# Layer 1 of the last two token blocks: eight of sixteen channel tiles by seven half products

## The chip, the core and the metric

The kernel runs on one core of a Trainium2 chip. The metric is the time of one execution on the device, in microseconds (us). The kernel before has a median of 338.77 us over three runs (338.13 to 338.88). A profile is one further execution with its trace.

## What is computed

Causal attention over 8 batches of 8 heads, 576 tokens and 64 features a head, with 16 beacon keys ahead of each sequence; then a low-rank mix along the sequence, and a two-layer perceptron on each token:

```python
scores = scale * np.matmul(q, k_all.transpose(0, 1, 3, 2))     # causal mask, softmax
x = softmax(scores) @ v_all                                    # (8, 576, 512) by tokens
h = x.transpose(0, 2, 1) @ U @ V                               # rank 32, along the sequence
u = x + h.transpose(0, 2, 1)
ch = np.maximum(u @ w_ch1, 0.0) @ w_ch2                        # 512 -> 2048 -> 512
return (u + ch).astype(np.float32)
```

Only the perceptron is touched: `u @ w_ch1` with the maximum is called layer 1 here, the product with `w_ch2` layer 2. Operands on the chip are 16-bit floats, sums are 32-bit.

## The kernel before

**Tiling.** The 8 x 576 = 4608 tokens go through the perceptron in nine blocks of 512 (`t` = 0 to 8). `uT` holds u with features on the partitions (4 tiles of 128), `w1` the weights of layer 1 (4 feature tiles by 2048 channels), so 16 channel tiles `dc` come out. Layer 1 of a block is 16 units (`g_unit`, L600): four matmuls of 128 weights by 512 tokens accumulate in one PSUM bank `gps` (L607), and the maximum with zero moves the bank into `gT` as 16-bit, on ScalarE for twelve of the units (L618) and on VectorE for the units 2, 5, 11 and 13 (L616).

**Layer 2** of blocks 1 to 8 is a 2 by 2 by 2 product of halves by seven products instead of eight (`product`, L627): `gT` is seen as four quarters (tokens halves of 256, channel halves of eight tiles), `sums` (L589) makes the four sums of quarters s1 to s4 on VectorE, `wt` holds four differences of `w2` quarters, and the seven products land in the banks A, F, B, C, D, E and D again, 16 matmuls of 256 columns each (L633), 112 for a block. Each product is two units (`c_unit`, L719). `SUMS` (L979) says after which unit each piece of the sums is issued. `after` (L668) joins the banks: one copy on ScalarE (L670), additions on VectorE (L654), the residual on GpSimd (also L654, `eng=nc.gpsimd`), and a store.

**Order.** Every engine's order is the order in which the program issues (`manual_schedule`). The units wait in one `queue`; `fill(n)` (L995) issues the next n of them between the steps of the attention, and with each unit it takes one entry of `coming` (L1004), a list of GpSimd's loads. For p = 12 to 31 (p is a pair of heads, four a batch) `long_slot` (L1198) writes out which scores, masks, attention products and units follow each other. After p = 31 `mix(B - 1)` (L1268) issues the rest of block 6 with the last mix, and the blocks 7 and 8, which are fed only then, run from L1273 on with nothing of the attention between them. `guard` (L813) and `guard_sum` (L825) check the softmax sums; `guard_sum` stands 22 units ahead of the end.

**Banks.** `pst` (L108) takes the bank that was emptied the longest time ago of eight; `emptying` gives one back.

**Staging.** `qk_tiles` (L253) takes two tiles of 6 KB a partition (`st0`, `st1`) from a pool with two buffers each: one batch's keys and queries lie there until they are turned by transposes on SyncE's queue. Batch 7's are the last.

Of the kernel before, what the change touches and what calls it, by code (L numbers as in the profile page):

```python
# [9 lines left out]
F16 = mybir.dt.float16  # L10
BF16 = mybir.dt.bfloat16
F32 = mybir.dt.float32
I32 = mybir.dt.int32
AF = mybir.ActivationFunctionType
ALU = mybir.AluOpType
# [3 lines left out]
P = 128  # L19
# [11 lines left out]
def kernel(  # L31
# [13 lines left out]
    nc = tc.nc  # L45
    B, H, S, D = q.shape
    Nb = beacon_k.shape[2]
    DM = H * D
    R = moe_U.shape[1]
    FF = moe_w_ch1.shape[1]  # L50
    NCC = DM // P
    NDC = FF // P
# [12 lines left out]
    TJ = 6  # L65
# [27 lines left out]
    stage = ctx.enter_context(tc.tile_pool(name="stage", bufs=2))  # L93
# [14 lines left out]
    def pst(shape, dtype, name):  # L108

        b = emptied.pop(0)  # L110
        t = psum.tile(shape, dtype, tag=f"bank{b}", name=name)
        bank_of[id(t)] = (b, t)
        return t

    def emptying(t):
        emptied.append(bank_of.pop(id(t))[0])
# [34 lines left out]
    w1 = const.tile([P, NCC, FF], F16, name="w1", tag="w1")  # L151
# [5 lines left out]
    plain = w1[:, NCC - 1, FF - P : FF]  # L157
# [4 lines left out]
    RING = 4 * S  # L162
    uT = const.tile([P, NCC, RING], F16, name="uT", tag="uT")
# [7 lines left out]
    HF, HC, HT = NDC // 2, DM // 2, 256  # L171
# [392 lines left out]
            for h in range(2) for o, x, y in ((t1, b12, b11), (t3, b22, b12), (t2, b22, t1), (t4, b21, t2))  # L564
        ]

    def fast_units(t0, dst, last=False):


        cell, banks, obs = {}, {}, {}  # L570
        cols = u_cols(t0, 512)

        def begin():
            t = gtp.tile([P, NDC * 512 + 3 * HF * HT], F16, name="gT", tag="gT")
            g = t[:, 0 : NDC * 512].rearrange("p (d t) -> p d t", t=512)
            s = t[:, NDC * 512 :].rearrange("p (i d t) -> p i d t", i=3, t=HT)
            cell["g"] = g
            cell["a"] = [g[:, 0:HF, 0:HT], g[:, HF:NDC, 0:HT], g[:, 0:HF, HT:512], g[:, HF:NDC, HT:512]]
            cell["s"] = [s[:, 0], s[:, 1], g[:, 0:HF, HT:512], s[:, 2]]
            ut = utp.tile([P, 4, DM], F16, name="ut", tag="ut")  # L580
            cell["u"] = ut
            cell["turns"] = [
                lambda cc=cc, at=at, o=o, w=w: nc.sync.dma_start_transpose(
                    out=ut[:, ds(o // P, w // P), ts(cc, P)], in_=uT[:, cc, ds(at, w)]
                )
                for cc in range(NCC) for at, o, w in cols
            ]
# [12 lines left out]
        def g_unit(k):  # L600
            if k == 0:
                begin()
            dc = order[k]
            g = pst([P, 512], F32, name="gps")
            for cc in range(NCC):
                for at, o, w in cols:
                    nc.tensor.matmul(  # L607
                        g[:, ds(o, w)], w1[:, cc, ts(dc, P)], uT[:, cc, ds(at, w)],
                        start=(cc == 0 and o == 0), stop=(cc == NCC - 1), skip_group_check=len(cols) > 1,
                    )  # L610
            if k % 2 and cell["turns"]:
                cell["turns"].pop(0)()
            for x in SUMS.get(k, ()):
                sums(*x)
            if k in (2, 5, 11, 13):
                nc.vector.tensor_scalar_max(out=cell["g"][:, dc, :], in0=g, scalar1=0.0)  # L616
            else:
                nc.scalar.activation(out=cell["g"][:, dc, :], in_=g, func=AF.Relu)  # L618
            emptying(g)

        b11, b21, b22 = w2[:, 0:HF, 0:HC], w2[:, HF:NDC, 0:HC], w2[:, HF:NDC, HC:DM]
        t1, t2, t3, t4 = (wt[:, i, :, :] for i in range(4))

        def pieces(bank):
            return [(0, 0, HC), (1, 0, P), (1, P, P)] if last and bank == "D" else [(0, 0, HC), (1, 0, HC)]
# [93 lines left out]
        def c_unit(k, j):  # L719
            bank = products[k][0]  # L720
            p = pieces(bank)[j]
            product(*products[k], *p)
            for x in SUMS.get(NDC + 2 * k + j, ()):
                sums(*x)
            if k == 6 and last:
                i, c0, w = p
                o = obs["12"][:, i, ds(c0, w)]
                add(o, banks["D", i, c0], cell["w12"][:, i, ds(c0, w)])
                store("12", 0, 1, i, c0, w)
                emptying(banks.pop(("D", i, c0)))  # L730
            elif j == len(pieces(bank)) - 1:
                after(k)

        units = [lambda k=k: g_unit(k) for k in range(NDC)]
        units += [lambda k=k, j=j: c_unit(k, j) for k in range(7) for j in range(len(pieces(products[k][0])))]
        return units

# [95 lines left out]
    NP = B * NH2  # L833
    NBLK = B * S // 512
    Ls, qTs, xbs = {}, {}, {}
    coming, storing = [], []

    def load_batch(b):
        if b < DT0:
            Ls[b] = qk_tiles()  # L840
            emit_loads(b, Ls[b], vss[b % 2])
        else:
            coming.append(lambda: v_beacon(beacon_v[b], vss[b % 2]))
            coming.extend(lambda j=j: v_tokens(v[b], vss[b % 2], ALLH, [j]) for j in range(NT))
# [114 lines left out]
    def av_of(p):  # L959
# [16 lines left out]
    LAG = 10  # L976
    HINT = 5
    FAST = 1
    SUMS = {  # L979
# [28 lines left out]
    def feed(b):  # L1008

        while state["t"] < NBLK and 512 * (state["t"] + 1) <= S * (b + 1):  # L1010
            t = state["t"]
            dst = lambda i, m, t=t: rows[ds(512 * t + P * i, m), :]
            if t < FAST:
                units, state["part"] = mlp_units(512 * t, 512, dst, t % 2, t > 0)
                if t == FAST - 1:
                    for i, u in zip(DIFFS, halves_of_w2()):
                        units[i] = lambda a=units[i], u=u: (a(), u())
            else:
                units = fast_units(512 * t, dst, t == NBLK - 1)
            queue.extend(units)  # L1020
            state["t"] += 1

# [39 lines left out]
    with tc.manual_schedule(engines={ENG.PE, ENG.Activation, ENG.DVE, ENG.SP, ENG.Pool}):  # L1062
# [9 lines left out]
        t0, sc = qkT_of(0), scores_of(0)  # L1072
# [35 lines left out]
        t2, t3 = qkT_of(2), qkT_of(3)  # L1108
# [17 lines left out]
        head, begin, rest = first_mix(xbs[0])  # L1126
        feed(0)
        part = state["part"]
# [121 lines left out]
        for p in range(NP1, NP):  # L1250
            b, c = divmod(p, NH2)
            if c == (1 if b >= DT0 else 0) and b + 1 < B:
                load_batch(b + 1)
            if c == (1 if b + 1 == DT0 else 2) and DT0 <= b + 2 < B:
                load_whole(b + 2)
            qk = qkT_of(p + 2) if P6 <= p and p + 2 < min(NP, DT0 * NH2) else []
            if p == P6:
                turn_x(b - 1)
                mix_between(b - 1)
            if c == 0 and DT0 <= b + 1 < B:  # L1260
                tr = turns(b + 1)
                fill_turns(tr, len(tr))
            if p < P6:
                play(third[c])
            else:
                long_slot(p, c, av_of(p), qk or [lambda: None] * 2)
# [60 lines left out]
    with tc.If(n_bad != 0, label="general"):  # L1327
        with tc.For_i(0, B, 1) as bi:
# [14 lines left out]
            for t0 in range(0, S, 512):  # L1343
                n = min(512, S - t0)
# [32 lines left out]
```

## Time and profile before

| | |
|---|---|
| median of 3 runs | 338.77 us |
| the profiled execution | 338.48 us |
| its span, first to last instruction | 336.8 us |
| granted TensorE clock, mean | 0.998 |
| block 7: layer 1, layer 2 | from 279.30, from 293.11 us |
| block 8: layer 1, layer 2 | from 305.34, from 319.35 us |
| last matmul ends | 331.6 us |

In the lines of the profile, PE is TensorE's matmuls, PEld its weight loads (they overlap PE), DVE is VectorE, ACT is ScalarE, POOL is GpSimd, SP is SyncE. A group line reads: line, engine, operation, output<-input, shapes, count | busy us, mean ns of one | idle time of the engine ahead of them and what ended it. A chain line reads: start, length, engine, tile, line, count. A timeline line reads: start, us, engine, line, operation, tiles, shapes, count, and in brackets the idle time before and its releaser. A window line reads: window, its length, busy us (and instructions) of PE, PEld, DVE, ACT and POOL, granted clock, share and rate of the DMA engines. The end of a matmul is modelled, so its own length (273 or 380 ns) is not the spacing of two matmuls; the spacing is read from starts.

### The profile page before, as it was taken

To read this page: it belongs to the slowest core of one execution; us is meant where nothing else is said; L and a number is where in the kernel's file an instruction comes from. 1 tells how busy PE (TensorE), PEld (TensorE's weight loads), DVE (VectorE), ACT (ScalarE), POOL (GpSimd) and SP (SyncE) were. 2 spreads that over 40 slices of the span, in tenths; PEclk is the share of its full clock that TensorE was granted. 3 is DMA by queue.
4 is the path that set the end of the run, shared out by engine and by line. 5 is a ranking of instruction groups with operands and counts; after the bars stand their busy time and mean duration, and the time that the engine had idled before them with its cause. 6 is when DMAs were issued, how large, how long until landed. Compare 5 with 4: busy or idle time off the path is not lost.

```text
span 336.8 us, 8862 instructions
## 1 busy us (share of the span) xinstructions
PE 328.0 (97%) x3542; PEld 216.5 (64%) x3542; DVE 234.3 (70%) x532; ACT 186.3 (55%) x403; POOL 141.2 (42%) x179
## 2 busy tenths in 40 slices
PE   8899999999999999999999999999999999999993
PEld 3565555555577557865688878656875675585493
DVE  6676888678897767775876587687776963733652
ACT  5957952888963677167716773577445303402500
POOL 8987714765335630786068706040140013013041
PEclk9999999999999999999999999999999999999999
DMA  7999999999999994999999999965123304004003
GB/s 165 142 182 155 174 200 189 200 186 137 85 167 137 130 182 89 139 206 144 166 112 157 153 120 123 138 127 101 35 80 81 70 33 140 16 33 140 18 33 102
DMA packets 150529, 41.98 MB, mean 125 GB/s; under 512 B 131280, under 2 KB 149904, under 8 KB 150480
## 3 DMA queue, kind: packets, MB, share of 16 engines
q0 software_dynamic: 87568, 18.18, 76.0%
q1 hardware_dynamic: 62688, 22.86, 36.2%
q8 instruction: 29, 0.48, 0.6%
q10 hardware_dynamic: 224, 0.30, 0.3%
q14 instruction: 20, 0.16, 0.2%
HBM read 37.45 MB, written 9.44 MB: 139 GB/s over the span
## 4 chain that ended last, share of the span: by engine, by line
PE 89%; ACT 5%; DVE 2%; DMA 1%; issue 0%; ACTq 0%; DVEq 0%
PE gps L607 32%; PE mpsD L633 8%; PE po L427 8%; PE sps L409 6%; PE mpsF L633 4%; PE cps L781 4%; PE mpsC L633 4%; PE mpsB L633 4%; PE mpsA L633 4%; PE gps L755 4%; PE mpsE L633 4%; ACT expt L376 2%; ACT w L376 2%; PE tps L298 1%; DMA stkq<-in_k_dram 1%; PE sps L370 1%
## 5 line engine op out<-in xcount | busy, mean ns | idle before, releaser
L607 PE MATMUL gps<-uT,w 128*128 128x512 f16 (+1 forms) x576 | 120.0, 356 | 0.2 <-ACT kT L907 0.2
L418 ACT ACTIVATE expt<-sps 128x496 f16<-128x496 f32 (+2 forms) x192 | 82.2, 547 | 41.6 <-PE sps L409 41.6
L654 POOL TENSOR_TENSOR ob<-ob,ut 128x512 f32<-128x512 f32 x30 | 36.0, 1203 | 143.9 <-DVE ob L654 134.7
L633 PEld LDWEIGHTS <-gT 128*128 128x128 f16 x912 | 85.5, 98 | 13.2 <-issue 2.9
L618 ACT ACTIVATE gT<-gps 128x512 f16<-128x512 f32 x96 | 57.2, 613 | 61.1 <-PE gps L607 55.8
L607 PEld LDWEIGHTS <-w 128*128 128x128 f16 x576 | 52.9, 98 | 46.4 <-issue 2.5
L596 DVE TENSOR_TENSOR gT<-gT 128x1024 f16<-128x1024 f16 (+2 forms) x88 | 45.3, 540 | 4.2 <-ACT gT L618 3.3
L240 POOL DMA_DIRECT2D vs<-in_v_dram x50 | 39.8, 811 | 14.0 <-DMA w<-in_moe_w_ch_dram 11.2
L427 PEld LDWEIGHTS <-expt 128*128 128x128 f16 x900 | 33.8, 98 | 9.8 <-issue 1.5
L616 DVE TENSOR_SCALAR gT<-gps 128x512 f16<-128x512 f32 x32 | 22.1, 690 | 24.2 <-PE gps L607 23.7
L427 PE MATMUL po<-vs,expt 128*128 128x65 f16 x900 | 36.4, 194 | 0.3
L348 DVE TENSOR_TENSOR expt<-expt,bigmask 128x768 f16<-128x768 f16 x54 | 33.9, 667 | 1.4 <-ACT expt L418 1.2
L436 DVE TENSOR_TENSOR xb<-po,rec 128x320 f16<-128x320 f32 x64 | 31.4, 491 | 2.2
L435 DVE RECIPROCAL rec<-po 128x5 f32<-128x5 f32 x64 | 12.1, 189 | 19.4 <-PE po L427 19.1
L409 PE MATMUL sps<-qT,kT 64*128 64x80 f16 (+4 forms) x288 | 22.6, 281 | 0.0
L376 ACT ACTIVATE expt<-sps 128x496 f16<-128x496 f32 (+2 forms) x48 | 20.4, 569 | 0.6 <-PE sps L370 0.6
L854 POOL DMA_DIRECT2D st<-in_q_dram x20 | 16.9, 871 | 7.7 <-DVE ob L654 6.8
L409 PEld LDWEIGHTS <-kT 64*128 64x128 f16 x288 | 10.3, 94 | 12.7 <-issue 8.2
L854 POOL DMA_DIRECT2D st<-in_k_dram x20 | 16.9, 859 | 0.6 <-DMA st<-in_q_dram 0.6
L755 PE MATMUL gps<-uT,w 128*128 128x512 f16 x64 | 16.2, 380 | 0.1
L633 PE MATMUL mpsE<-wt,gT 128*128 128x256 f16 x128 | 16.2, 273 | 0.0
L633 PE MATMUL mpsB<-wt,gT 128*128 128x256 f16 x128 | 16.1, 273 | 0.0
(121 smaller groups left out, 350.5 us busy)
## 6 DMA issues: line engine op xcount, KB each, us to landing
out_dram<-ob SPq DMA_DIRECT2D x35, 256.0 KB, 2.9
vs<-in_v_dram POOLq DMA_DIRECT2D x18, 128.0 KB, 6.6
w<-in_moe_w_ch_dram POOLq DMA_DIRECT2D x4, 512.0 KB, 6.2
w<-in_moe_w_ch_dram POOLq DMA_DIRECT2D x2, 1024.0 KB, 12.3
st<-in_k_dram POOLq DMA_DIRECT2D x12, 128.0 KB, 6.7
st<-in_q_dram POOLq DMA_DIRECT2D x12, 128.0 KB, 7.3
st<-in_k_dram POOLq DMA_DIRECT2D x4, 288.0 KB, 11.8
st<-in_q_dram POOLq DMA_DIRECT2D x4, 288.0 KB, 12.5
```

The lines of the kernel that those rows point to most:

```text
L240: nc.gpsimd.dma_start(out=dst[a : a + nq[j], j, :, :], in_=src[hs, ds(q0[j], nq[j]), :].rearrange("h p d -> p h d"))
L348: nc.vector.tensor_tensor(out=e, in0=e, in1=bigmask[:, :, :].rearrange("p (a b) x -> p a b x", b=2), op=ALU.min)
L376: nc.scalar.activation(out=ex[i][:, ds(AT[g], gw[g])], in_=ps[g, i][:, 0 : gw[g]], func=AF.Exp, scale=scale)
L409: nc.tensor.matmul(banks[i][:, ds(at0 + o, w)], kT(hp, c, ch), qT[hp, c, ds(qa, w)], start=True, stop=True, skip_group_check=len(unit) > 1,)
L418: nc.scalar.activation(out=at[p][3][i][:, ds(AT[g], gw[g])], in_=bank[:, ds(at0, gw[g])], func=AF.Exp, scale=scale)
L427: nc.tensor.matmul(po[:, j, :], ex[0 : nk[c], ds(blk[(c, j)], P)], vs[0 : nk[c], ds(c * H * E + h * E, E)], start=(c == 0), stop=(c == j),)
L596: nc.vector.tensor_tensor(out=o[:, ds(d0, n)], in0=x[:, ds(d0, n)], in1=y[:, ds(d0, n)], op=op)
L607: nc.tensor.matmul(g[:, ds(o, w)], w1[:, cc, ts(dc, P)], uT[:, cc, ds(at, w)], start=(cc == 0 and o == 0), stop=(cc == NCC - 1), skip_grou ...
L618: nc.scalar.activation(out=cell["g"][:, dc, :], in_=g, func=AF.Relu)
L633: nc.tensor.matmul(ps, a()[:, d, ds(P * i, P)], bm[:, d, ds(c0, w)], start=fresh and d == 0 and (i == 0 or key != bank), stop=d == HF - 1, ...
L654: eng.tensor_tensor(out=out, in0=x, in1=y, op=ALU.add)
L854: coming.append(lambda d=dst, s=src, a=m[j] - nq[j], n=m[j], j=j: nc.gpsimd.dma_start(out=d[a:n, j, :, :], in_=s[:, ds(q0[j], nq[j]), :].r ...
```

## The change

Layer 1 of the blocks 7 and 8 (`QUADS`) is issued in another form. Eight of the sixteen channel tiles stay whole units (`plain`, all emptied by ScalarE). The tiles 0 to 3 and 8 to 11 form two sets q = 0, 1: tiles 2q, 2q+1 with 8+2q, 9+2q. Each set is a 2 by 2 by 2 product of halves (features, channel pairs, tokens), made of seven half products of four matmuls of 256 columns (`half`). The sums of w1's quarters are made once, by GpSimd, as eight entries of `coming` at p = 29; the four differences of uT's quarters are made for each block by VectorE (`us`), and are shared by both sets. They lie in `lw`, two tiles that take the staging tiles' buffers; three ScalarE copies a set, in 32 bits, lie in `lk`, in the other buffers. The maximum with zero of these tiles is partly on ScalarE and partly on VectorE, in place. The order of the fifteen units of layer 1 is `slots`; the pieces of layer 2's sums are issued at other units (`late`, `after_g`). Blocks 0 to 6 are issued as before.

```diff
@@ -564,7 +564,32 @@
             for h in range(2) for o, x, y in ((t1, b12, b11), (t3, b22, b12), (t2, b22, t1), (t4, b21, t2))
         ]
 
-    def fast_units(t0, dst, last=False):
+    lq = {}
+
+    def quad_tiles():
+
+        t = [stage.tile([P, TJ * DM], F16, name=f"lw{i}", tag=f"st{i}") for i in range(2)]
+        lq["w"] = [x[:, 0 : 4 * 512].rearrange("p (k c f) -> p k c f", k=4, c=2) for x in t]
+        lq["t"] = [x[:, ds(4 * 512 + 512 * k, 512)].rearrange("p (c x) -> p c x", c=2) for x in t for k in range(2)]
+        f = [stage.tile([P, 3, 512], F32, name=f"lk{i}", tag=f"st{i}") for i in range(2)]
+        lq["k"] = [[x[:, k, :].rearrange("p (i x) -> p i x", i=2) for k in range(3)] for x in f]
+
+    def quad_weights(q):
+
+        def part(c0, d):
+            return w1[:, ds(c0, 2), ds(P * d, 2 * P)]
+
+        a11, a12, a21, a22 = part(0, 2 * q), part(2, 2 * q), part(0, HF + 2 * q), part(2, HF + 2 * q)
+        s1, s2, s3, s4 = (lq["w"][q][:, k, :, :] for k in range(4))
+        return [
+            lambda o=o, x=x, y=y, op=op: nc.gpsimd.tensor_tensor(out=o, in0=x, in1=y, op=op)
+            for o, x, y, op in (
+                (s1, a21, a22, ALU.add), (s2, s1, a11, ALU.subtract),
+                (s3, a11, a21, ALU.subtract), (s4, a12, s2, ALU.subtract),
+            )
+        ]
+
+    def fast_units(t0, dst, last=False, quads=False):
 
 
         cell, banks, obs = {}, {}, {}
@@ -617,6 +642,102 @@
             else:
                 nc.scalar.activation(out=cell["g"][:, dc, :], in_=g, func=AF.Relu)
             emptying(g)
+
+        def g_quads():
+
+            at = t0 % RING
+            b11, b12, b21, b22 = (uT[:, ds(c, 2), ds(at + x, HT)] for c in (0, 2) for x in (0, HT))
+            t1, t2, t3, t4 = lq["t"]
+            us = [
+                lambda o=o, x=x, y=y: nc.vector.tensor_tensor(out=o, in0=x, in1=y, op=ALU.subtract)
+                for o, x, y in ((t1, b12, b11), (t2, b22, t1), (t3, b22, b12), (t4, b21, t2))
+            ]
+            held = {}
+
+            def plain(k, dc):
+                if k == 0:
+                    begin()
+                g = pst([P, 512], F32, name="gps")
+                for cc in range(NCC):
+                    nc.tensor.matmul(
+                        g, w1[:, cc, ts(dc, P)], uT[:, cc, ds(at, 512)], start=cc == 0, stop=cc == NCC - 1
+                    )
+                nc.scalar.activation(out=cell["g"][:, dc, :], in_=g, func=AF.Relu)
+                emptying(g)
+
+            def half(q, bank, a, b, fresh):
+                if fresh:
+                    held[q, bank] = pst([P, 2, HT], F32, name="qps" + bank)
+                for i in range(2):
+                    for c in range(2):
+                        nc.tensor.matmul(
+                            held[q, bank][:, i, :], a(c, i), b[:, c, :], start=fresh and i == 0 and c == 0,
+                            stop=c == 1, skip_group_check=True,
+                        )
+
+            def of_w1(c0, d):
+                return lambda c, i: w1[:, c0 + c, ts(d + i, P)]
+
+            def of_lw(q, k):
+                return lambda c, i: lq["w"][q][:, k, c, ts(i, P)]
+
+            def copied(q, k):
+                nc.scalar.activation(out=lq["k"][q][k], in_=held[q, "A"], func=AF.Copy)
+
+            def summed(q, bank, k, d, x):
+                nc.vector.tensor_tensor(
+                    out=cell["g"][:, ds(d, 2), ds(x, HT)], in0=held[q, bank], in1=lq["k"][q][k], op=ALU.add
+                )
+
+            def relu(o):
+                nc.vector.tensor_scalar_max(out=o, in0=o, scalar1=0.0)
+
+            def step(q, n):
+                d, e = 2 * q, HF + 2 * q
+                if n == 0:
+                    half(q, "A", of_w1(0, d), b11, True)
+                    copied(q, 0)
+                    half(q, "F", of_w1(2, d), b21, True)
+                    summed(q, "F", 0, d, 0)
+                    emptying(held.pop((q, "F")))
+                    relu(cell["g"][:, ds(d, 2), 0:HT])
+                elif n == 1:
+                    half(q, "A", of_lw(q, 1), t2, False)
+                    copied(q, 1)
+                    half(q, "D", of_lw(q, 0), t1, True)
+                elif n == 2:
+                    half(q, "A", of_lw(q, 2), t3, False)
+                    copied(q, 2)
+                    summed(q, "D", 2, e, HT)
+                else:
+                    half(q, "A", of_w1(2, e), t4, False)
+                    nc.scalar.activation(out=cell["g"][:, ds(e, 2), 0:HT], in_=held[q, "A"], func=AF.Relu)
+                    emptying(held.pop((q, "A")))
+                    half(q, "D", of_lw(q, 3), b22, False)
+                    summed(q, "D", 1, d, HT)
+                    emptying(held.pop((q, "D")))
+                    relu(cell["g"][:, :, HT:512].rearrange("p (h d) t -> p h d t", h=2)[:, :, ds(d, 2), :])
+
+            slots = [4, 12, 5, (0, 0), (1, 0), (0, 1), (1, 1), 13, (0, 2, 1, 2), 6, 14, (0, 3), (1, 3), 7, 15]
+            late = {12: ((0, 4, 3),), 13: ((1, 4, 3), (2, 4, 3)), 14: ((0, 0, 4), (1, 0, 4))}
+
+            def unit(k, slot):
+                if isinstance(slot, int):
+                    plain(k, slot)
+                else:
+                    for i in range(0, len(slot), 2):
+                        step(slot[i], slot[i + 1])
+                if k < len(us):
+                    us[k]()
+                if k % 2 and cell["turns"]:
+                    cell["turns"].pop(0)()
+                for x in late.get(k, ()):
+                    sums(*x)
+
+            return [lambda k=k, slot=slot: unit(k, slot) for k, slot in enumerate(slots)]
+
+        after_g = {0: ((0, 7, 1), (1, 7, 1)), 1: ((2, 0, 4), (2, 7, 1)), 2: ((3, 0, 4),), 3: ((3, 4, 4),)}
+        sums_at = after_g if quads else {k - NDC: x for k, x in SUMS.items()}
 
         b11, b21, b22 = w2[:, 0:HF, 0:HC], w2[:, HF:NDC, 0:HC], w2[:, HF:NDC, HC:DM]
         t1, t2, t3, t4 = (wt[:, i, :, :] for i in range(4))
@@ -720,7 +841,7 @@
             bank = products[k][0]
             p = pieces(bank)[j]
             product(*products[k], *p)
-            for x in SUMS.get(NDC + 2 * k + j, ()):
+            for x in sums_at.get(2 * k + j, ()):
                 sums(*x)
             if k == 6 and last:
                 i, c0, w = p
@@ -731,7 +852,7 @@
             elif j == len(pieces(bank)) - 1:
                 after(k)
 
-        units = [lambda k=k: g_unit(k) for k in range(NDC)]
+        units = g_quads() if quads else [lambda k=k: g_unit(k) for k in range(NDC)]
         units += [lambda k=k, j=j: c_unit(k, j) for k in range(7) for j in range(len(pieces(products[k][0])))]
         return units
 
@@ -976,6 +1097,7 @@
     LAG = 10
     HINT = 5
     FAST = 1
+    QUADS = (7, 8)
     SUMS = {
         8: [(0, 0, 4)], 9: [(1, 0, 4)], 10: [(2, 0, 4)], 12: [(3, 0, 4)],
         14: [(0, 4, 3)], 15: [(1, 4, 3)], 16: [(2, 4, 3)], 17: [(0, 7, 1), (1, 7, 1)],
@@ -1016,7 +1138,7 @@
                     for i, u in zip(DIFFS, halves_of_w2()):
                         units[i] = lambda a=units[i], u=u: (a(), u())
             else:
-                units = fast_units(512 * t, dst, t == NBLK - 1)
+                units = fast_units(512 * t, dst, t == NBLK - 1, t in QUADS)
             queue.extend(units)
             state["t"] += 1
 
@@ -1251,6 +1373,9 @@
             b, c = divmod(p, NH2)
             if c == (1 if b >= DT0 else 0) and b + 1 < B:
                 load_batch(b + 1)
+            if p == NP - 3:
+                quad_tiles()
+                coming.extend(quad_weights(0) + quad_weights(1))
             if c == (1 if b + 1 == DT0 else 2) and DT0 <= b + 2 < B:
                 load_whole(b + 2)
             qk = qkT_of(p + 2) if P6 <= p and p + 2 < min(NP, DT0 * NH2) else []
```

## The prediction

> **What bounds the kernel now.** I read the page first, then the end of the chain of waits in order of time, then busy time by windows for the two blocks that change.
>
> ```profile
> span 336.8 us, 8862 instructions
> PE 328.0 (97%) x3542; PEld 216.5 (64%) x3542; DVE 234.3 (70%) x532; ACT 186.3 (55%) x403; POOL 141.2 (42%) x179
> ...
> PE 89%; ACT 5%; DVE 2%; DMA 1%; issue 0%; ACTq 0%; DVEq 0%
> ```
>
> TensorE is busy for 97% of the span and is 89% of the chain that ends last. The part that the change touches is the end of that chain:
>
> ```profile
> 277.39 1.91 PE mpsD L633 x16
> 279.30 13.81 PE gps L607 x64
> 293.11 1.75 PE mpsA L633 x16
> ...
> 305.34 8.63 PE gps L607 x40
> 314.06 5.29 PE gps L607 x24
> 319.35 1.75 PE mpsA L633 x16
> ...
> 329.85 1.78 PE mpsD L633 x24
> ```
>
> From 277.39 us on every link is TensorE and each starts where the one before ends: 54 us in which nothing else decides. So a matmul that isn't issued there is worth its whole spacing, as long as no other engine becomes late. The windows show how much the others have in hand:
>
> ```profile
> 279.30:293.10 13.80, 13.80 (x66) 6.29 (x65) 6.89 (x11) 6.57 (x11) 1.53 (x2) 1.00 0.34 95
> 293.10:305.30 12.20, 12.20 (x114) 10.91 (x112) 5.52 (x11) 1.19 (x2) 3.15 (x3) 1.00 0.11 37
> ```
>
> In layer 1 of block 7 VectorE (6.89 us) and ScalarE (6.57 us) work half of the 13.80 us. In layer 2 the weight loads take 10.91 of 12.20 us and are still covered: PE shows no gap.
>
> **The spacing of matmuls.** 64 matmuls of 512 columns take 13.81 us: 0.2158 us each. The 112 of 256 columns in block 7's layer 2 run from 293.11 to 305.34: 12.23 / 112 = 0.1092 us each. That is more than half of 0.2158, by a little; the rest is a price per matmul, and the seven-for-eight trade pays it on more matmuls. Before, a set of four channel tiles is 16 matmuls of 512 columns, 16 x 0.2158 = 3.453 us. After, it is 7 x 4 = 28 of 256 columns, 28 x 0.1092 = 3.058 us. A set saves 0.395 us, a block 0.79 us, and the four sets 1.58 us. Break-even would be a spacing of 3.453 / 28 = 0.1233 us. The half products have the same shape, the same 16-bit weights of 128 columns and the same alternation inside one bank as layer 2's products, so I take 0.1092; below 0.1079 (half of 0.2158) no row goes, which would add 28 x 4 x 0.0013 = 0.15 us to the gain.
>
> A rule speaks against this. The Trainium skill, "TensorE: Matmul & The Clock Gate", section "Back-to-back issue gap", gives sustained spacings of 81 ns for 128 columns and 131 ns for 512; on the straight line between them 256 columns would be an estimate of 98 ns, a set would go from 16 x 131 = 2096 to 28 x 98 = 2744 ns, and four sets would lose 2.6 us. The trace's 215.8 ns for 512 columns contradicts it and agrees with the formula of the same section that the page calls isolated (N / 2.4 + 2.5 ns: 215.8 and 109.2), so the sum stands by the rows.
>
> **Does TensorE stay unbroken in layer 1?** Durations of the work that is added or moved:
>
> ```profile
> L618 ACT ACTIVATE gT<-gps 128x512 f16<-128x512 f32 x24 | 14.3, 597 | 35.9 <-PE gps L607 35.9
> L596 DVE TENSOR_TENSOR gT<-gT 128x1024 f16<-128x1024 f16 x10 | 6.8, 685 | 3.4 <-ACT gT L618 3.3
> L616 DVE TENSOR_SCALAR gT<-gps 128x512 f16<-128x512 f32 x8 | 5.5, 693 | 10.1 <-PE gps L607 10.1
> ...
> L596 DVE TENSOR_TENSOR gT<-gT 128x768 f16<-128x768 f16 x6 | 3.2, 555 | 0.3
> ...
> L596 DVE TENSOR_TENSOR gT<-gT 128x256 f16<-128x256 f16 x6 | 1.6, 290 | 0.1
> L654 DVE TENSOR_TENSOR ob<-mpsF,kept 128x512 f32<-128x512 f32 x2 | 1.4, 692 | 3.2 <-PE mpsF L633 3.2
> L670 ACT ACTIVATE kept<-mpsA 128x512 f32<-128x512 f32 x2 | 1.2, 597 | 2.4 <-PE mpsA L633 2.4
> ```
>
> ScalarE goes from 12 to 16 instructions of 0.60 us a block (8 whole tiles, 6 copies, 2 maxima), 9.6 us in a layer 1 of 8 x 0.863 + 14 x 0.437 = 13.02 us (a whole tile is 4 x 0.2158, a half product 4 x 0.1092). VectorE loses four of 0.693 us and gains six sums of a bank and a copy (0.692 us each, by the L654 row), four differences of 512 elements (between 0.290 and 0.555 us; I take 0.42) and four maxima in place, two of 512 and two of 1024 elements. No row has a maximum in place on 16-bit data: nearest are a copy of 768 elements below, at 0.436 us, and the subtraction of 1024 at 0.685 us, so 0.29 to 0.69; I take 0.35 and 0.53, by the copy's time per element. (The Trainium skill, "VectorE: DVE Perf Modes", perf-mode tier table, puts such an operation in a mode of four elements a cycle, an estimate of 0.42 us for 1024 with its fixed 150 cycles; no run here shows it, and the sum would not change.)
>
> ```profile
> L291 DVE COPY pr<-st 96x768 f16<-96x768 f16 x18 | 7.7, 436 | 0.2
> ...
> 297.58 1.15 POOL L654 TENSOR_TENSOR ob<-ob,ut 128x512 f32<-128x512 f32 x1 [16.25 <-DVE ob L654]
> ...
> 280.25 0.60 ACT L618 ACTIVATE gT<-gps 128x512 f16<-128x512 f32 x1 [12.26 <-PE gps L607]
> 281.06 0.60 ACT L618 ACTIVATE gT<-gps 128x512 f16<-128x512 f32 x1 [0.22 <-PE gps L607]
> ...
> 292.22 2.98 DVE L596 TENSOR_TENSOR gT<-gT 128x768 f16<-128x768 f16 x7
> 296.81 0.69 DVE L654 TENSOR_TENSOR ob<-mpsF,kept 128x512 f32<-128x512 f32 x1 [1.61 <-PE mpsF L633]
> ```
>
> ScalarE starts some 0.05 us behind a unit's last matmul (281.06 against 279.30 + 2 x 0.863 = 281.03). With T the start of layer 1, four places could stop TensorE, which waits in order with everything behind it:
>
> - *Bank A, second product.* A is copied before the next half product may add to it. Tiles 4, 12 and 5 end at T+2.59, A of set 0 at 3.03, its F at 3.46, A and F of set 1 at 4.34; then A of set 0 is wanted. ScalarE has tile 5 until 3.24 and the copy until 3.84: 0.5 us in hand. The copy of set 1 ends at 4.55, wanted at 5.21: 0.66. In block 7 these two copies carry some dozen waits for batch 7's long finished transfers each. VectorE's sum of bank F, with four waits, starts 0.20 us behind its product (296.81 against 293.11 + 2 x 1.75 = 296.61), 0.15 us more than ScalarE needs with one: some 0.05 us a wait, 0.6 us a copy, and I suppose that they are passed behind tile 5's start at 2.64, while that instruction runs. Nothing to 0.5 us, once; I take nothing.
> - *Bank A, third product* and *bank D, second product.* A is wanted at 6.95 against a copy by 5.5; the sums that read D run from 8.3 to 9.7 and D is wanted at 9.98 and 10.86. Over 1 us in hand.
> - *Layer 2's first product* reads tiles 0 to 7 of the first token half: tile 7, the last of them, is out at 12.80, wanted at 13.02 or later.
> - *The sums for layer 2's third product.* The last two D sums move VectorE's end: D of set 0 ends at 10.42, so sum 10.5 to 11.2, maximum to 11.75, sum to 12.45, maximum to 13.0. Then seven subtractions or additions are due (three of 768, two of 1024, two of 256 elements, 3.6 us one by one; before it was seven in 2.98 us): the two of 1024 are done by 16.0, the last at 16.6. The product starts at 13.02 + 4 units of 0.874 = 16.51 with the tiles of the first, and reads the last tile 7 x 0.109 later. 0.5 us in hand, 0.2 with the dearer maxima. Before the change it had 1.4 us (295.20 against 293.11 + 3.50 = 296.61), so this is the thinnest cover. If it is gone, every 0.1 us beyond is paid in both blocks. I take nothing.
>
> The differences of uT are done by about T+2 in VectorE's idle time, before A's second product at 4.34. Later VectorE work (the other sums, F's addition) slips by some 2 us and is back in step by the fourth product; the banks that it empties are not taken again in that phase.
>
> **The weight sums on GpSimd.** Eight additions of 512 16-bit pairs, where the trace has only 32-bit ones of 1.15 us (at 297.58 above) or, contended, 1.40 us (below), and no shorter two-input row; I take 1.15, between 0.7 and 1.4. They are issued one by one behind the units of p = 29, between the residuals of block 5's layer 2 (timelines of VectorE, GpSimd and TensorE):
>
> ```profile
> 219.43 2.83 DVE L348 TENSOR_TENSOR expt<-expt,bigmask 128x768 f16<-128x768 f16 x2 [0.24 <-ACT expt L418]
> 236.06 1.02 DVE L348 TENSOR_TENSOR expt<-expt,bigmask 128x768 f16<-128x768 f16 x2
> 248.50 1.98 DVE L348 TENSOR_TENSOR expt<-expt,bigmask 128x768 f16<-128x768 f16 x2
> ...
> 254.01 1.03 DVE L348 TENSOR_TENSOR expt<-expt,bigmask 128x768 f16<-128x768 f16 x2 [0.24 <-ACT expt L418]
> ...
> 219.25 4.02 POOL L654 TENSOR_TENSOR ob<-ob,ut 128x512 f32<-128x512 f32 x3 [8.99 <-DVE gT L616]
> 239.49 1.16 POOL L654 TENSOR_TENSOR ob<-ob,ut 128x512 f32<-128x512 f32 x1 [16.23 <-DVE ob L654]
> 246.11 1.15 POOL L654 TENSOR_TENSOR ob<-ob,ut 128x512 f32<-128x512 f32 x1 [5.46 <-DVE ob L654]
> 248.66 1.40 POOL L654 TENSOR_TENSOR ob<-ob,ut 128x512 f32<-128x512 f32 x1 [1.40 <-DVE ob L654]
> ...
> 250.23 0.61 PE L427 MATMUL po<-vs,expt 128*128 128x65 f16 x15
> ```
>
> In GpSimd's order the first stands ahead of the residual of 239.49, the next six behind it, the eighth behind that of 246.11. So it takes the first at 223.3 us, when its three residuals are done, and six from 240.65 to 247.5. The residual of 246.11 moves to 247.5, the eighth sum and two residuals follow to about 252. This isn't free for VectorE: two masks take 1.02 us alone, 1.98 and 2.83 us beside GpSimd. The masks at 248.50 are beside it already, and may now take up to 2.83: 0.85 us more, with the first of them wanted at 250.23 (before, done near 249.5: 0.7 us in hand). The stores behind the moved residuals wait up to 1.4 us on SyncE's queue; nothing reads them. I take nothing, with nothing to 0.4 us as bounds; the sums are used 30 us later.
>
> **The sum.** Against the profiled execution, 336.8 us of span and 338.48 in all: 338.48 - 1.58 = 336.90. The median of before lies 0.29 us above that execution, so 338.77 - 1.58 = 337.19: I say 337.2. With the bounds together (0.15 more gained; 0.5 + 2 x 0.2 + 0.4 lost) it runs from 337.0 to 338.5.
>
> **Rivals.**
>
> - *The covers are too thin* (0.18). Each layer 1 loses to a copy or a late sum. By a ScalarE instruction's 0.60 us a block beyond the 0.5 in hand it would lose 0.1, by VectorE's 0.6 us of dearer operations on top of late starts about 0.4: 0.2 to 1.2 us for both blocks, 337.4 to 338.4; with 0.7 it is 337.9. For it: 0.2 to 0.5 us are all that is in hand. Against: ScalarE is idle for a quarter of layer 1.
> - *GpSimd's sums hold up the attention* (0.10), the case on the other side. A 16-bit addition may cost twice the 32-bit one, 2.3 us. Then six run to 254.5, the queue behind them to 260, and the masks at 248.50 and near 254 wait for one such instruction each: four waits of up to 1.15 us, less 0.7 in hand, are 3.9 us on TensorE: 337.2 + 3.9 = 341.1. It decides from 2.3 us of lost time on, that is from about 1.7 us an addition. Against: half the bytes, and no row above 1.40.
> - *Short runs of half products are spaced worse than layer 2's* (0.04). At 0.1233 us the gain is zero, 338.8; with a weight load of 98 ns laid bare once a half product the four sets lose 28 x 0.098 = 2.7 us, 339.9. It is the direction of the page's rule, at whose figures 338.77 + 2.6 = 341.4. Against: the gapless 112 matmuls from 293.11.
> - *The change doesn't do what it says*, where the staging isn't dead and the first sum waits for a transfer (0.02): it would have to be late by 30 us to be seen.
>
> **How the numbers follow.** The forecast has 0.66. About 0.2% (0.7 us) is what a measurement of this kernel tells from no change: faster is the forecast and two thirds of the first rival, 0.66 + 0.12 = 0.78; the same is its last third and half of the third and fourth, 0.09; slower is the second and the rest, 0.13. The range, 336.8 to 338.4, has the forecast with a run's scatter below it and the first rival above; it leaves the GpSimd case out.
>
> **What would show it.** Right: layer 1 of both blocks spans 13.0 us instead of 13.8 with no PE wait, PE's busy time falls by 1.6 us, and everything up to 279.30 is where it was. The half products' starts are 0.109 us apart. Thin covers would show as PE waits on bank A or D in layer 1, or on gT ahead of the bank B product. GpSimd's sums above 1.4 us, masks near 2.8 us and a layer 1 of block 7 that starts after 279.5 would show the second rival. I am wrong if the start of block 7 moves, or if either layer 1 is longer than 13.4 us.

## The result and the profile after

The changed kernel takes 337.14 us (median of 6 runs, 336.76 to 337.64), the kernel before 338.69 us beside it (6 runs, 338.13 to 339.17). The ratio is 0.9956, with a 95% interval of 0.9942 to 0.9969. The profiled execution has 337.18 us and a span of 335.4 us. The page's first lines, then the end of the chain of waits (start, length, engine, tile, line, count) and the two blocks by windows:

```profile
span 335.4 us, 9013 instructions
...
PE 326.7 (97%) x3590; PEld 221.5 (66%) x3590; DVE 241.4 (72%) x552; ACT 190.3 (57%) x411; POOL 150.3 (45%) x187
```

```profile
277.83 1.91 PE mpsD L754 x16
279.73 2.59 PE gps L662 x12
...
292.75 1.75 PE mpsA L754 x16
...
304.98 2.59 PE gps L662 x12
...
318.20 1.75 PE mpsA L754 x16
...
328.70 1.78 PE mpsD L754 x24
```

```profile
279.73:292.75 13.02, 13.02 (x91) 8.66 (x89) 8.62 (x16) 8.52 (x15) 1.65 (x2) 1.00 0.36 101
292.75:304.98 12.23, 12.23 (x114) 10.91 (x112) 8.22 (x16) 1.19 (x2) 3.19 (x3) 1.00 0.12 39
304.98:318.20 13.22, 13.22 (x92) 8.66 (x90) 8.67 (x17) 8.53 (x15) 1.54 (x2) 1.00 0.32 86
```

Layer 1 is 13.02 us in block 7 (before 13.81) and 13.22 in block 8 (before 319.35 - 305.34 = 14.01), with TensorE busy from end to end (block 8's holds the guard's matmul and is 0.2 us longer, as before). Each is 0.79 us shorter; layer 2 is as long as it was, 12.23 and 12.28 us. VectorE and ScalarE now work 8.6 and 8.5 us of the 13.02.

The span falls by 1.4 us and not by 1.58. Two small things stand between: block 7 starts 0.43 us later (279.73 against 279.30), and the stretch behind the last matmul is 0.25 us shorter (335.4 - 330.48 against 336.8 - 331.63). The 0.43 us are made in the start, long before the first of the added instructions, GpSimd's weight sum at 224.19 us. The chains before and after show it, each with the first product of an early layer 2:

```profile
94.99 1.75 PE mpsA L633 x16
```

```profile
95.43 1.75 PE mpsA L754 x16
```

From there to block 7 it is 184.31 us before (279.30 - 94.99) and 184.30 after (279.73 - 95.43): the attention with GpSimd's sums beside it takes as long as it did. Two loads go with the start's 0.44 us. One is that of the first values; this line of TensorE's list of waits after (waiter <- releaser: us in all, times, longest) is not in the list of before:

```profile
PE po L427 <- DMA vs<-in_v_dram: 0.4, 1, 0.4
```

By 22.6 us TensorE is 0.19 us behind the trace of before. The rest comes at 43.56 us, where a weight load on TensorE waits for a transfer of weights and before did not. The changed kernel, run again, has block 7 start at 279.59 and 279.27 us, 184.30 and 184.31 us behind the same product.

### The profile page after: what moved, and what is told of

It is laid out like the page before. It is cut to its first block, busy times and chain, and to the rows that moved or that the text cites. A ratio compares the mean times of both kernels' runs of the same rounds, so it can differ in the third digit from the quotient of the medians.

```text
span 335.4 us, 9013 instructions
## 1 busy us (share of the span) xinstructions
PE 326.7 (97%) x3590; PEld 221.5 (66%) x3590; DVE 241.4 (72%) x552; ACT 190.3 (57%) x411; POOL 150.3 (45%) x187
## 4 chain that ended last, share of the span: by engine, by line
PE 90%; DVE 2%; POOL 2%; DMA 2%; ACT 1%; issue 1%; POOLq 0%; DVEq 0%
PE gps L632 24%; PE po L427 9%; PE mpsD L754 8%; PE sps L409 6%; PE gps L876 4%; PE mpsF L754 4%; PE cps L902 4%; PE mpsC L754 4%; PE mpsB L754 4%; PE mpsA L754 4%; PE gps L662 4%; PE mpsE L754 4%; PE qpsA L673 2%; DMA vs<-in_v_dram 2%; PE tps L298 1%; PE sps L370 1%
## 5 line engine op out<-in xcount | busy, mean ns | idle before, releaser
L632 PE MATMUL gps<-uT,w 128*128 128x512 f16 (+1 forms) x448 | 91.9, 349 | 0.2 <-ACT kT L1028 0.2
L632 PEld LDWEIGHTS <-w 128*128 128x128 f16 x448 | 40.4, 98 | 31.9 <-issue 2.5
L643 ACT ACTIVATE gT<-gps 128x512 f16<-128x512 f32 x72 | 42.9, 619 | 25.2 <-PE gps L632 19.9
L348 DVE TENSOR_TENSOR expt<-expt,bigmask 128x768 f16<-128x768 f16 x54 | 31.5, 623 | 1.3 <-ACT expt L418 1.2
L641 DVE TENSOR_SCALAR gT<-gps 128x512 f16<-128x512 f32 x24 | 16.6, 691 | 15.7 <-PE gps L632 15.1
L665 ACT ACTIVATE gT<-gps 128x512 f16<-128x512 f32 x16 | 9.6, 597 | 28.4 <-PE gps L662 28.4
L409 PE MATMUL sps<-qT,kT 64*128 64x80 f16 (+4 forms) x288 | 22.6, 281 | 0.0
```

The costliest lines, as they stand in the source:

```text
L348: nc.vector.tensor_tensor(out=e, in0=e, in1=bigmask[:, :, :].rearrange("p (a b) x -> p a b x", b=2), op=ALU.min)
L409: nc.tensor.matmul(banks[i][:, ds(at0 + o, w)], kT(hp, c, ch), qT[hp, c, ds(qa, w)], start=True, stop=True, skip_group_check=len(unit) > 1,)
L632: nc.tensor.matmul(g[:, ds(o, w)], w1[:, cc, ts(dc, P)], uT[:, cc, ds(at, w)], start=(cc == 0 and o == 0), stop=(cc == NCC - 1), skip_grou ...
```

## The experiments

Each changes one thing. Where no other is named, the diff stands against the changed kernel; `...` marks lines left out. Beside the experiments the kernel before has medians of 339.15 to 339.23 us, and 338.69 beside the first result, so ratios are compared and not times of different sets.

**Only the weight sums.** Layer 1 is issued as before, GpSimd makes the sums.

```diff
-    QUADS = (7, 8)
+    QUADS = ()
```

> GpSimd's eight weight sums stay at p = 29, layer 1 of the blocks 7 and 8 is issued as before (nothing uses the sums). If the gain is TensorE's alone and the sums are covered: the time of before, 338.7 us (ratio 0.999 to 1.001), block 7's layer 1 13.81 us long, starting within 0.1 us of where the kernel before has it, once the start of the attention is the same. If the sums cost time beside the attention (GpSimd theory): 339.1 us or more, with the layer 1 of block 7 starting later by the same.

Measured: 339.14 us against 339.23 before, ratio 0.9998 (0.9985 to 1.0012). Block 7's layer 1 runs from 279.47 to 293.28, 13.81 us. From the early product at 95.16 us it starts 184.31 us later, as before. The sums alone cost nothing that shows.

**One block.**

```diff
-    QUADS = (7, 8)
+    QUADS = (8,)
```

> Only block 8's layer 1 is issued as half products. If each block pays on its own by its matmuls: half the gain, 0.79 us, 337.9 us (ratio 0.9977), layer 1 of block 7 13.81 us and of block 8 13.02 us and the guard's 0.2. If the gain came from something shared (GpSimd's or SyncE's order, a changed tail): nearer to 337.1 or to 338.7 us.

Measured: 338.28 us against 339.23, ratio 0.9960 (0.9929 to 0.9990); the forecast 0.9977 is inside, but so is the whole gain, 0.9956. The chain tells them apart:

```profile
279.81 13.81 PE gps L632 x64
293.63 1.75 PE mpsA L754 x16
...
305.86 2.59 PE gps L662 x12
...
319.07 1.75 PE mpsA L754 x16
```

Block 7 is as before (13.82 us), block 8 has 13.21 instead of 14.01. So block 8 gains its 0.80 us with block 7 unchanged: a block pays by itself.

**Eight products instead of seven.** Eight whole tiles are computed in matmuls of 256 columns, and GpSimd makes no sums.

```diff
-                    nc.tensor.matmul(
-                        g[:, ds(o, w)], w1[:, cc, ts(dc, P)], uT[:, cc, ds(at, w)],
...
+                    for x in (0, HT) if t0 // 512 in SPLIT and dc % HF < 4 else (None,):
+                        o1, w_, at1 = (o, w, at) if x is None else (o + x, HT, at + x)
+                        nc.tensor.matmul(
+                            g[:, ds(o1, w_)], w1[:, cc, ts(dc, P)], uT[:, cc, ds(at1, w_)],
...
-    QUADS = (7, 8)
+    QUADS = ()
+    SPLIT = (7, 8)
...
-                coming.extend(quad_weights(0) + quad_weights(1))
+                pass
```

> Eight of sixteen channel tiles in the blocks 7 and 8 are whole tiles as before, but each matmul of 512 columns is two of 256 (eight products where the change has seven); no sums of weights or tokens, no copies. If the gain is one product of eight less, and a matmul costs 0.0013 us on top of its columns: layer 1 is 32 x 0.2158 + 64 x 0.1092 = 13.89 us, 0.08 longer than before, 338.9 us in all (0.17 more). If short matmuls themselves were the gain: below 338.4 us; if runs of them cost more than layer 2's 0.1092: layer 1 above 14.0 us.

Measured: 339.05 us against 339.23, ratio 0.9991 (0.9966 to 1.0015), too wide for 0.17 us. The chain has it to the hundredth:

```profile
279.29 13.89 PE gps L634 x96
293.18 1.75 PE mpsA L757 x16
```

96 matmuls take 13.89 us. So shape alone loses 0.08 us a block, and one product of eight left out is worth 0.08 + 0.79 = 0.87 us a block, 8 matmuls of 0.1092 us.

**The weight sums twice.**

```diff
+            for _ in range(2)
         ]
...
-                coming.extend(quad_weights(0) + quad_weights(1))
+                both = quad_weights(0) + quad_weights(1)
+                coming.extend(lambda i=i: (both[2 * i](), both[2 * i + 1]()) for i in range(8))
```

> The changed kernel, with each of the eight weight sums made twice (the same result), as if an addition took 2.3 us. By the price of the prediction's rival (masks wait four times for up to 1.15 us, less 0.7 in hand) TensorE loses 3.9 us: 341 us. By the theory that VectorE's masks are held only by the one GpSimd instruction that they meet, and that the first of them has 0.7 us in hand: 337.1 to 338.0 us, block 7's layer 1 not later by more than 0.9 us.

Measured: 337.21 us against 339.23, ratio 0.9955 (0.9932 to 0.9977): nothing lost. Timelines of GpSimd and VectorE (start, us, engine, line, operation, tiles, shapes, count, idle before):

```profile
253.04 2.73 POOL L585 TENSOR_TENSOR lw<-w 128x512 f16<-128x512 f16 x2
```

```profile
248.71 2.13 DVE L348 TENSOR_TENSOR expt<-expt,bigmask 128x768 f16<-128x768 f16 x2
...
254.21 1.99 DVE L348 TENSOR_TENSOR expt<-expt,bigmask 128x768 f16<-128x768 f16 x2 [0.24 <-ACT expt L418]
```

GpSimd is at one pair of sums from 253.04 to 255.77 us and at the last from 257.17 to 259.55. Both pairs of masks are held: 2.13 us (1.98 in the changed kernel) and 1.99 us (1.03). But each pair is late by 1 us at most, and TensorE loses nothing: block 7 starts at 279.50, 184.31 us behind the early product at 95.19, as before. For a queue of sums that is twice as long, the prediction's price of 3.9 us was far too high. It let four masks wait 1.15 us each in a row and took only 0.7 us off for all of them, while each pair has its own time in hand. Two instructions of 1.15 us are not one of 2.3, though: a mask that met one longer instruction might be held for longer, and no run tried that.

**The last maxima three times.**

```diff
-            def relu(o):
-                nc.vector.tensor_scalar_max(out=o, in0=o, scalar1=0.0)
+            def relu(o, n=1):
+                for _ in range(n):
+                    nc.vector.tensor_scalar_max(out=o, in0=o, scalar1=0.0)
...
-                    relu(cell["g"][:, :, HT:512].rearrange("p (h d) t -> p h d t", h=2)[:, :, ds(d, 2), :])
+                    relu(cell["g"][:, :, HT:512].rearrange("p (h d) t -> p h d t", h=2)[:, :, ds(d, 2), :], 3)
```

> The changed kernel with VectorE's two last maxima of a layer 1 (1024 elements, in place) made three times each, the same result. In the changed kernel's trace the fifth of the seven sums for layer 2's third product ends near 295.3 us and that product starts at 296.25: 0.9 us in hand. Four more maxima of about 0.46 us, each behind the one before, are 1.84 us: if the cover is as read, TensorE waits some 0.9 us ahead of the bank B product in both blocks, 1.8 us more in all (span 337.2), layer 1 unchanged at 13.02 us. If other VectorE time is in hand there: no wait.

Measured, in one execution: span 338.4 us, 3.0 more than the changed kernel's (0.1 of it ahead of block 7, 0.2 behind the last matmul). VectorE, then the windows of block 7's two layers, then TensorE's waits in both blocks:

```profile
291.03 1.35 DVE L694 TENSOR_SCALAR gT<-gT 128x1024 f16<-128x1024 f16 x3
...
293.01 1.35 DVE L694 TENSOR_SCALAR gT<-gT 128x1024 f16<-128x1024 f16 x3
294.27 5.48 DVE L621 TENSOR_TENSOR gT<-gT 128x768 f16<-128x768 f16 x11
```

```profile
279.85:292.86 13.01, 13.01 (x90) 8.66 (x89) 8.58 (x16) 8.53 (x15) 1.65 (x2) 1.00 0.36 101
292.86:306.18 13.32, 12.41 (x114) 10.85 (x112) 9.96 (x20) 1.20 (x2) 3.20 (x3) 1.00 0.11 36
```

```profile
PE mpsB L755 <- DVE gT L621: 2.3, 2, 1.4
```

With T the start of layer 1, the sums start at T + 14.42 (294.27 - 279.85) instead of T + 12.59 (292.32 - 279.73): 1.83 us later, as expected. Layer 1 keeps 13.01 us, and block 7's bank B product starts 0.9 us late, at 297.27. So 0.93 us were in hand. Layer 2 of block 7 then has 13.32 us instead of 12.23: 0.9 ahead of the bank B product and 0.2 inside it. Block 8's wait is longer, 1.4 us, which was not expected.

**The copies of bank A two and three times.** The diff is for two; for three it says `range(3)`.

```diff
-                nc.scalar.activation(out=lq["k"][q][k], in_=held[q, "A"], func=AF.Copy)
+                for _ in range(2):
+                    nc.scalar.activation(out=lq["k"][q][k], in_=held[q, "A"], func=AF.Copy)
```

> The changed kernel with each ScalarE copy of bank A made twice, the same result: 22 instead of 16 ScalarE instructions a layer 1. They follow each other every 0.49 us in the changed kernel's trace (282.36, 282.85). By the cover worked out in the prediction (0.5 us at the first copy): the first copy's second run ends at T+4.2, bank A is wanted at T+4.34; the second's at T+5.2, wanted at T+5.21: no wait or below 0.2 us in all, layer 1 13.0 to 13.1 us. If the copies bound the phase (the rival of thin covers): 0.6 us a block or more.

> The changed kernel with each ScalarE copy of bank A made three times: 28 ScalarE instructions every 0.49 us are 13.7 us in a layer 1 of 13.02. If ScalarE's cover is what keeps TensorE unbroken: waits on bank A at its second and third products, 2.0 to 2.5 us a block by the same steps, 4 to 5 us in all (span 339.4 to 340.4). If ScalarE is not near the path: no more than 1 us in all.

Measured, in one execution each: spans of 336.7 and 343.7 us. Both cost more than I expected. The windows of block 7's layer 1, first two times, then three times:

```profile
279.87:293.41 13.54, 13.40 (x90) 8.63 (x89) 8.54 (x16) 11.35 (x21) 1.65 (x2) 1.00 0.35 97
```

```profile
279.43:296.74 17.31, 14.07 (x91) 8.60 (x89) 8.62 (x16) 14.94 (x27) 1.65 (x2) 1.00 0.27 76
```

With two, layer 1 is 13.54 us, 0.52 more. ScalarE's timeline says why:

```profile
282.50 0.60 ACT L665 ACTIVATE gT<-gps 128x512 f16<-128x512 f32 x1 [0.27 <-PE gps L662]
282.99 4.58 ACT L686 ACTIVATE lk<-qpsA 128x512 f32<-128x512 f32 x8
```

I had taken 0.49 us, the step from a maximum to a copy (282.50, 282.99), for every step. Read one by one, the copies start at 282.99, 283.61, 284.11 and 284.73: a repeat comes 0.62 us behind the copy that it repeats, when that has ended, and the next set's copy 0.50 behind the repeat. In the changed kernel, where no copy is repeated, two copies one behind the other keep the short step (1.08 - 0.60 = 0.48):

```profile
287.21 1.08 ACT L685 ACTIVATE lk<-qpsA 128x512 f32<-128x512 f32 x2
```

So the first copy's second run ends at 284.21 and not at T + 4.2 = 284.07, and TensorE starts at 284.26 where it would have started at 284.05. The second copy's ends at 285.33, and TensorE starts at 285.38, which would have been 284.92. With three times, ScalarE is the bound: it works 14.94 of 17.31 us, the chain runs through its copies from 284.32 to 293.65, and TensorE waits for it (both blocks):

```profile
PE qpsA L673 <- ACT lk L686: 6.0, 8, 1.2
```

So the cover on ScalarE is real: one more run of each copy costs 0.5 us a block, two cost 4.3. My sum for three times, 2.0 to 2.5 us a block, was half of what came.

**Block 6 as well** (three_blocks). The weight sums are issued at p = 27, and the last mix is put one unit earlier in the queue, which keeps its place.

```diff
-    QUADS = (7, 8)
+    QUADS = (6, 7, 8)
...
-        n = 0 if not turned else LAG + 3 if b == B - 1 else min(LAG, len(queue) - 8)
+        n = 0 if not turned else LAG + 2 if b == B - 1 else min(LAG, len(queue) - 8)
...
-            if p == NP - 3:
+            if p == 27:
```

> Block 6's layer 1 is issued as half products too, amid the last attention pairs (weight sums at p = 27, one unit fewer ahead of the last mix). TensorE's own saving is 0.79 us more than the changed kernel: 336.3 us if the others stay covered (ratio to before 0.993). Against it: in that stretch VectorE works 12.3 of 16.1 us and would get 4.4 us more, with masks, attention sums and the guard in its order: it needs 16.7 us in 15.3, and some 1 to 2 us of TensorE waits would leave 336.8 to 338.3 us.

Measured: 338.00 us against 339.19 before, ratio 0.9964 (0.9953 to 0.9976). That is inside the 336.8 to 338.3 us of the expectation's second half, and no more than the changed kernel's gain (0.9956, with an interval that overlaps). VectorE, then TensorE:

```profile
264.28 0.49 DVE L943 TENSOR_REDUCE allg<-good 128x1 f32<-128x320 f16 x1
...
264.87 0.68 DVE L688 TENSOR_TENSOR gT<-qpsD,lk 128x512 f16<-128x512 f32 x1
...
266.99 5.48 DVE L621 TENSOR_TENSOR gT<-gT 128x768 f16<-128x768 f16 x11
```

```profile
269.98 1.92 PE L754 MATMUL mpsB<-wt,gT 128*128 128x256 f16 x16 [0.76 <-DVE gT L621]
```

The guard's operations stand in VectorE's order ahead of the last D sums; these start at 264.87, though the first of their banks was done near 263. Block 6's bank B product starts 0.92 us late (the row has 0.76 of idle time, as the end of the matmul before it is modelled).

**Block 6, with the guard's operations given out** (three_blocks_guard). The diff is against the kernel above; the guard's operations are cut into five steps, its tile lies in another pool, and the steps go out with the units of block 7's layer 2.

```diff
...
-        guard()
+        at = len(queue) - 31 - 14 + 7
+        for i, u in enumerate(guard()):
+            queue[at + i] = lambda a=queue[at + i], u=u: (a(), u())
```

> As three_blocks, with the guard's nine VectorE operations (261 to 265 us there) given out over the units of block 7's layer 2. In three_blocks TensorE waits 0.92 us ahead of block 6's bank B product, behind sums that VectorE starts at 267.0 us, after the guard and the late D sums. If that queue is the cause: the wait is gone or below 0.2 us, layers 1 of the blocks 7 and 8 stay 13.02 and 13.2 us, and the kernel is 0.7 to 0.8 us faster than the changed kernel in the same rounds (ratio to before near 0.993). If the attention's own VectorE work is the cause: the wait stays above 0.5 us and the time is that of three_blocks.

> The changed kernel itself beside three_blocks_guard, on the same chip: 1.58 us less than before by the theory (ratio 0.9953), layers 1 of 13.02 and 13.22 us again.

Measured: 336.86 us (ratio to before 0.9939, 0.9919 to 0.9960), and 337.10 us for the changed kernel (0.9940, 0.9922 to 0.9959). The wait is gone (the D sums start at 262.54, the bank B product at 268.43 without one), so the guard's place in VectorE's queue was its cause. The gain over the changed kernel is smaller than expected, so both ran once more:

> three_blocks_guard once more, beside the changed kernel: its trace has block 7's layer 1 0.81 us earlier, its median was only 0.24 us lower, with the runs of both overlapping. If the trace's difference is what it is worth: 0.6 to 0.9 us below the changed kernel's median. If something behind the last matmul or in the start gives it back: within 0.3 us.

> The changed kernel beside guard_b: the same as in the rounds before, ratio to before 0.994 to 0.9956.

Measured: 337.09 us (0.9943, 0.9923 to 0.9963) and 337.46 us (0.9947, 0.9928 to 0.9965). The chains of these two are 0.01 us apart up to 95 us (94.97 and 94.96), so they can be compared directly, three_blocks_guard first:

```profile
94.97 1.75 PE mpsA L754 x16
...
265.11 1.75 PE mpsA L754 x16
278.79 2.59 PE gps L662 x12
```

```profile
94.96 1.75 PE mpsA L754 x16
...
265.58 1.75 PE mpsA L754 x16
279.27 2.59 PE gps L662 x12
```

Block 6 gives 0.47 us by the start of its layer 2, and not 0.79. The rest is lost inside its layer 1, where in three_blocks_guard a half product starts 0.55 us behind the one before instead of 0.44 (254.59, 255.14), and an attention product 1.05 us behind the start of a whole tile of 0.87 (256.88, 257.93). Medians of 0.24 and 0.37 us less go with that. The 0.37 lies between the two expectations, above what was said for a gain given back and below the 0.6 to 0.9. The intervals of the ratios overlap: it is the fastest version that was run, by a difference that these runs do not prove.

## Why the prediction was right

**The spacing of matmuls.** It carried the whole gain: 13.02 us a layer 1 was forecast and measured. Half products follow each other at the same spacing as layer 2's products:

```profile
282.16 0.60 PE L673 MATMUL qpsA<-uT,w 128*128 128x256 f16 x4
282.60 0.60 PE L673 MATMUL qpsF<-uT,w 128*128 128x256 f16 x4
283.03 0.60 PE L673 MATMUL qpsA<-uT,w 128*128 128x256 f16 x4
```

Eight matmuls are issued in 0.87 us (283.03 - 282.16), 0.109 each. The rival of worse-spaced short runs falls by these rows. The Trainium skill, "TensorE: Matmul & The Clock Gate", section "Back-to-back issue gap", gives sustained spacings by which, as the prediction worked out, the change would lose. Its 131 ns for 512 columns stand against 215.8 ns here (64 in 13.81 us, before). Eight products in the same shape gain nothing, so it is the product left out that pays.

**Bank A.** The first copy was forecast for T + 3.24 to 3.84 and ran from T + 3.12 to 3.71 (282.85, 0.59 us):

```profile
282.36 0.60 ACT L665 ACTIVATE gT<-gps 128x512 f16<-128x512 f32 x1 [0.27 <-PE gps L662]
282.85 0.59 ACT L685 ACTIVATE lk<-qpsA 128x512 f32<-128x512 f32 x1
```

The dozen waits on finished transfers show no cost: in block 8, where the copies carry none of them, the same step is also 0.49 us (307.61, 308.10). TensorE starts the next product on that bank at 283.91, 0.47 us after the copy ended (283.44), so some 0.5 us were in hand, as forecast.

**The sums for layer 2's third product.** The forecast had 0.5 us in hand; it was 0.93. The term that was mis-sized is VectorE's: the maxima of 1024 and 512 elements take 0.43 and 0.29 us instead of 0.53 and 0.35, and the next operation starts 0.34 us after a maximum:

```profile
290.92 0.43 DVE L693 TENSOR_SCALAR gT<-gT 128x1024 f16<-128x1024 f16 x1
291.26 0.68 DVE L688 TENSOR_TENSOR gT<-qpsD,lk 128x512 f16<-128x512 f32 x1
291.98 0.43 DVE L693 TENSOR_SCALAR gT<-gT 128x1024 f16<-128x1024 f16 x1
292.32 5.48 DVE L621 TENSOR_TENSOR gT<-gT 128x768 f16<-128x768 f16 x11
```

The 0.43 us agrees with the estimate of 0.42 that the prediction worked out from the Trainium skill, "VectorE: DVE Perf Modes", perf-mode tier table, better than with my reading from the copy's row. F's addition and the ones behind it slip and are back in step at 299.78, the fourth product's (bank C), as forecast.

**The weight sums.** 1.15 us each was taken and is what seven of the eight took, as long as a 32-bit addition; the one beside the masks, at 248.94, took 1.56:

```profile
224.19 1.15 POOL L585 TENSOR_TENSOR lw<-w 128x512 f16<-128x512 f16 x1
239.93 1.16 POOL L775 TENSOR_TENSOR ob<-ob,ut 128x512 f32<-128x512 f32 x1 [14.59 <-DVE ob L775]
```

The masks beside them take 1.98 us, the same as before. The rival of GpSimd failed at its condition, as the addition is not dearer. The argument against it was half right: half the bytes gained nothing. Its price was wrong for a longer queue, as the doubled sums show.

**The differences of uT** were forecast for T + 2 at 0.42 us each. Three take 0.42, but the second takes 1.26 us beside a residual on GpSimd (280.61 to 281.88), so three are done by T + 2.8. The fourth stands behind the sum of the first bank F in VectorE's order and ends at 284.83, T + 5.1: there the forecast was wrong. It does not matter, as the sums of the prediction put the first product that reads one of the three at T + 4.34, and the first that reads the fourth at T + 9.55:

```profile
280.45 0.42 DVE L652 TENSOR_TENSOR lw<-uT 128x512 f16<-128x512 f16 x1
280.90 1.26 DVE L652 TENSOR_TENSOR lw<-uT,lw 128x512 f16<-128x512 f16 x1
```

**The time.** 337.2 us was said and 337.14 measured; the difference of medians is 1.55 us for 1.58. That the two times agree to less than 0.1 us is partly luck, as single runs of the changed kernel lie 0.9 us apart; that each layer 1 lost 0.79 us is not. The prediction named a moved start of block 7 as a sign against it. The start did move, by 0.43 us, but ahead of 95.43 us and so not by the change; the sign should have been the stretch from an early product, which is the same to 0.01 us. PE's busy time falls by 1.3 us for the same reason: by 1.6 from block 7 on, as forecast, with 0.3 more in the first 95 us.

## What to carry to other kernels

Where the chain of waits is one engine without a gap, the price of a change is its instructions by their spacing, read from starts in the same trace, and the rest of the work is to ask at each hand-over how much time the other engines have in hand. A cover, the time that an engine has in hand before another waits for it, is measured by spending it: an operation that can be repeated with the same result, done two or three times, tells how much was left. It told here that VectorE has 0.9 us and ScalarE 0.5 us in hand. The price of the repeat itself has to be read from its own trace, as a repeat can follow more slowly than other work. The same change put into a busier stretch gave 0.47 of 0.79 us in one pair of traces, and only after work that nobody was waiting for had been moved out of the queue ahead of it.

## What was not expected of the hardware

A copy on ScalarE that repeats the one before it starts 0.62 us behind it, when it has ended; a copy of the other set's bank starts 0.48 to 0.50 us behind, ahead of the other's end. The repeat reads the same bank and writes the same tile; which of the two holds it was not tried. On VectorE it is alike: an in-place maximum repeated three times takes steps of 0.46 us (1.35 for three, 0.43 for one), and the next sum starts 0.34 us behind a single one. With the maxima made three times, block 8's wait ahead of bank B was 1.4 us against block 7's 0.9, though VectorE's sums were equally late; only in block 8 does the read of the guard's flag stand in TensorE's order behind the first weight load of that product. It takes 0.49 us from 323.8, and the product starts at 324.31; this fits, but whether it is the cause was not tried.
